# Order of the input and weight loads in a fused gated-attention and ReGLU kernel, and the planner's account of its DMA queues

## The chip, the core and the metric

The kernel runs on one core of a Trainium2 chip. The engines are named as in the profile: PE (matrix products), DVE and ACT (element-wise work; both read the matrix results in PSUM), POOL (element-wise work in SBUF, and the queue of the weight loads) and SP (the queue of all other transfers). The metric is device time in microseconds (us), the median of several runs. One further execution was profiled, and all durations below come from it.

## The reference, cut to what matters

For 4 batches, 8 heads, 768 steps and head width 48, a state of 48x48 decays by a gate of its own for each row, takes up an outer product, and is read by the query. The result, 3072 tokens of 384 numbers, goes through a ReGLU network of 384 to 1536 to 384.

```python
f = 1.0 / (1.0 + np.exp(-f_logit))
for t in range(S):
    state = f[:, :, t, :, None] * state + np.einsum('bhd,bhe->bhde', k[:, :, t], v[:, :, t])
    y[:, :, t] = np.einsum('bhd,bhde->bhe', q[:, :, t], state)
x = y.transpose(0, 2, 1, 3).reshape(B * S, H * D)
out = (np.maximum(x @ w_gate, 0.0) * (x @ w_val)) @ w_out
```

## The kernel before

**Units.** The 3072 tokens are cut into 24 chunks of 128. Two neighbouring chunks of one batch are a unit; there are 12 units, and `seq` (line 399) sets their order: units 0 to 3 are the first 256 tokens of the four batches, 4 to 7 the next, 8 to 11 the last. A unit needs four loads of 384 KB, f, k, q and v (`load`, line 572). Four buffers of each kind exist, so unit 4 loads into the buffers of unit 0.

**Attention of one unit** (`unit`, line 652). ACT takes the exponential and the logarithm of f (lines 669, 671); PE sums the logs over time (678, 679); ACT takes exponentials of the sums (690, 693, 700); DVE or POOL multiply k and q by them ("hats", 712, 718). The hats are turned either by PE (770, copied to `qkT` by DVE or ACT; units in `pe_hats`) or by a DMA transpose (792). PE makes scores (806), which are masked into `ptm` by DVE (820), or by an ACT copy (815) and a POOL product (817). v is spread into `vpad` (753). PE makes the state's increment (860 or 871), DVE and POOL update the state (638, 643, 646), and PE makes the output (904 or 915), which is copied, or copied and turned by a DMA, into `xT` (926, 932 to 934).

**The network** works on groups of four chunks (two units). `ffn_hidden` (line 940) makes, for one of 12 slices j of 128 hidden columns, the gate product (3 matmuls, line 956), its ReLU on ACT (958), the value product (960) and the product `gT` on DVE (964). `ffn_out` (line 969) multiplies by `w_out` (984). For group 0 the loop of line 1015 does some slices in two halves, chunks 0 and 1 (unit 0) first, then chunks 2 and 3 (unit 1), so that half of the work can begin when only unit 0 is done. Gate and value results share four PSUM banks (group "f" in line 463), so PE can be two slices ahead of ACT and DVE.

**The weights** are cast to bf16 on the way in, so POOL issues them (`load_w`, line 585): four slices each of `wg`, `wv` and `wo`, each of three hidden columns j, 288 KB written.

**The order of the work** is not written by hand: a list scheduler inside the kernel (`Plan.schedule`, line 192) has a cost and a priority for every operation and puts each engine's instructions in a fixed order when the kernel is built. On the chip each engine runs its list in order and waits on semaphores; if one instruction waits, everything behind it on that engine waits too. The class `Rings` (line 53) is the scheduler's account of the two DMA queues: `hw` is SP's, `sw` is POOL's. The list `first` (line 398) is the order of the first 16 input loads and 12 weight slices; `wg0@k1` means that the issue of wg0 waits until k1 has landed. A transfer after 30 us is planned as if it landed `op.slack` later (line 1014), a reserve. While PE is planned to wait before 24 us, it is given matmuls on zeros (line 1050; below: fillers) that keep it busy and give nothing.

Of the kernel before, what the change touches and what calls it, by code (L numbers as in the profile page):

```python
# [52 lines left out]
class Rings:  # L53


    CAP, LAND = 3300, 1.0
    RATE = {"hw": (1.0, 0.21), "sw": (1.0, 0.69)}
# [3 lines left out]
    def __init__(self):  # L61
        self.now = 0.0
        self.passed = 0
        self.coming = []
# [13 lines left out]
    def speed(self, ring):  # L78
        return self.RATE[ring][1 if self.queue[self.OTHER[ring]] else 0]

    def worked(self, t, ring):
        work = t - self.now
        if ring == "sw":
            return work
        for p in self.PAUSES[self.passed:]:
            if p >= t:
                break
            work -= max(0.0, min(t, p + self.PAUSE) - max(self.now, p))
        return work

    def later(self, work, ring):
        t = self.now
        if ring == "sw":
            return t + work
        for p in self.PAUSES[self.passed:]:
            if t + work <= p:
                break
            work -= max(0.0, p - t)
            t = max(t, p + self.PAUSE)
        return t + work  # L100

    def next(self):
        found = None
        for r, q in self.queue.items():
            if q:
                t = self.later(self.left[r] / self.speed(r), r)
                if found is None or t < found[0]:
                    found = (t, r)
        if self.coming and (found is None or self.coming[0][0] < found[0]):
            found = (self.coming[0][0], None)  # L110
        return found

    def step(self, t, ring):
        speeds = {r: self.speed(r) for r in self.RATE}
        for r, q in self.queue.items():
            if q:
                self.left[r] -= self.worked(t, r) * speeds[r]
        self.now = t
        while self.passed < len(self.PAUSES) and self.PAUSES[self.passed] + self.PAUSE <= t:
            self.passed += 1  # L120
        if ring is None:
            _, _, op = self.coming.pop(0)
            q = self.queue[op.ring]
            q.append(op)
            if len(q) == 1:
                self.left[op.ring] = op.flow
            return None
        op = self.queue[ring].pop(0)
        self.out[ring] -= op.descs
        if self.queue[ring]:  # L130
            self.left[ring] = self.queue[ring][0].flow
        return op


class Plan:
# [56 lines left out]
    def schedule(self, banks):  # L192
# [46 lines left out]
        while True:  # L239
# [130 lines left out]
def bass_hgrn2_outer__then__ffn_reglu_kernel(  # L370
# [53 lines left out]
    vrow = [sb(f"vrow{i}", [128, 2, HD], BF16) for i in range(2 if any(e.get("vpe") for e in {0: {'kps': False, 'qps': False, 'q0': 'POOL', 'q1': 'POOL', 'even': 'PE', 'm00': 'DVE', 'm01': 'DVE', 'm10': 'DVE', 'tk': 'DVE', 'm11': 'DVE', 'r1': 'POOL', 'tq': 'ACT', 'v11': 'ACT', 'v10': 'DVE', 'r0': 'ACT', 'v01': 'ACT', 'v00': 'DVE1', 'vb': 'DVE1', 'pr': False, 'o1': 'DVE', 'vc0': 'DVE', 'x0': 'ACT', 'x1': 'ACT', 'yy': True, 'o0': 'ACT', 'vc1': 'ACT'}, 1: {'kps': True, 'r0': 'ACT', 'm01': 'DVE', 'm00': 'DVE', 'tq': 'DVE', 'v11': 'POOL', 'even': 'PE', 'tk': 'ACT', 'q1': 'DVE', 'v00': 'DVE1', 'm11': 'POOL', 'r1': 'DVE', 'm10': 'DVE', 'v01': 'POOL', 'v10': 'POOL', 'q0': 'POOL', 'qps': False, 'yy': False, 'td': False, 'vb': 'DVE', 'vc0': 'DVE', 'o0': 'DVE', 'vc1': 'DVE', 'x0': 'ACT', 'o1': 'ACT'}, 2: {'tk': 'DVE', 'v01': 'POOL', 'kps': True, 'r1': 'ACT', 'r0': 'ACT', 'even': 'PE', 'q0': 'DVE', 'v00': 'POOL', 'v10': 'ACT', 'm00': 'DVE', 'v11': 'DVE1', 'm01': 'POOL', 'm11': 'POOL', 'tq': 'DVE', 'q1': 'POOL', 'm10': 'POOL', 'qps': True, 'x0': 'ACT', 'vc1': 'ACT', 'pr': False, 'vc0': 'DVE', 'o0': 'DVE', 'x1': 'ACT', 'vb': 'POOL'}, 4: {'v10': 'DVE1', 'v01': 'POOL', 'm00': 'DVE', 'q11': 'POOL', 'q00': 'POOL', 'q01': 'POOL', 'q0': 'POOL', 'kps': True, 'even': 'DVE', 'm01': 'DVE', 'v00': 'ACT', 'm10': 'POOL', 'q10': 'POOL', 'q1': 'POOL', 'm11': 'POOL', 'v11': 'DVE1', 'qps': False, 'tq': 'DVE', 'r0': 'ACT', 'tk': 'DVE', 'r1': 'ACT', 'yy': True, 'o1': 'ACT', 'o0': 'DVE', 'x1': 'DVE', 'x0': 'DVE'}, 10: {'m00': 'POOL', 'm10': 'POOL', 'q0': 'POOL', 'kps': True, 'q10': 'POOL', 'm01': 'POOL', 'q11': 'POOL', 'q00': 'POOL', 'v11': 'ACT', 'even': 'DVE', 'v01': 'DVE1', 'v00': 'POOL', 'q01': 'POOL', 'q1': 'POOL', 'm11': 'DVE', 'v10': 'ACT', 'td': True, 'o0': 'DVE'}, 9: {'v11': 'ACT', 'v10': 'ACT', 'even': 'DVE', 'kps': True, 'q1': 'POOL', 'm10': 'DVE', 'v00': 'ACT', 'm11': 'POOL', 'q11': 'POOL', 'm00': 'DVE', 'q00': 'POOL', 'q10': 'POOL', 'q0': 'POOL', 'q01': 'POOL', 'v01': 'DVE1', 'm01': 'DVE', 'yy': False, 'x0': 'DVE', 'td': True, 'o0': 'DVE'}, 3: {'kps': True, 'm00': 'DVE', 'm11': 'POOL', 'v11': 'DVE1', 'm10': 'POOL', 'tk': 'ACT', 'v01': 'DVE1', 'r1': 'DVE1', 'tq': 'DVE', 'q1': 'POOL', 'v00': 'DVE1', 'v10': 'POOL', 'q0': 'POOL', 'r0': 'DVE1', 'm01': 'DVE', 'even': 'DVE', 'qps': False, 'vb': 'DVE1', 'x1': 'ACT', 'o1': 'DVE', 'vc1': 'ACT', 'pr': False, 'vc0': 'DVE', 'o0': 'ACT'}, 5: {'q1': 'POOL', 'm00': 'DVE', 'kps': True, 'q11': 'POOL', 'v10': 'ACT', 'v00': 'DVE1', 'even': 'DVE', 'q01': 'POOL', 'm11': 'POOL', 'q00': 'POOL', 'q0': 'POOL', 'v11': 'POOL', 'm01': 'DVE', 'q10': 'POOL', 'v01': 'ACT', 'm10': 'DVE', 'tq': 'ACT', 'r0': 'DVE1', 'tk': 'DVE', 'r1': 'DVE1', 'qps': False, 'o1': 'ACT', 'x0': 'DVE', 'o0': 'ACT', 'yy': False}, 11: {'q0': 'POOL', 'v01': 'ACT', 'q10': 'POOL', 'm00': 'DVE', 'q01': 'POOL', 'm11': 'POOL', 'q1': 'POOL', 'q00': 'POOL', 'kps': True, 'v11': 'ACT', 'm01': 'DVE', 'q11': 'POOL', 'even': 'DVE', 'v00': 'DVE1', 'm10': 'POOL', 'v10': 'DVE1', 'yy': True, 'o1': 'DVE', 'td': True}, 7: {'v10': 'POOL', 'kps': True, 'q1': 'POOL', 'v01': 'POOL', 'q11': 'POOL', 'm00': 'DVE', 'v11': 'DVE1', 'even': 'PE', 'm10': 'POOL', 'm11': 'DVE', 'm01': 'POOL', 'q10': 'POOL', 'qps': False, 'q01': 'POOL', 'q0': 'POOL', 'o0': 'DVE', 'x1': 'DVE', 'td': True, 'x0': 'ACT', 'o1': 'ACT'}, 8: {'m10': 'DVE', 'v11': 'ACT', 'q01': 'POOL', 'm01': 'POOL', 'even': 'DVE', 'q0': 'POOL', 'v10': 'ACT', 'q1': 'POOL', 'm00': 'DVE', 'kps': True, 'q11': 'POOL', 'q00': 'POOL', 'qps': False, 'v00': 'DVE1', 'q10': 'POOL', 'v01': 'ACT', 'pr': False, 'td': True, 'x0': 'DVE'}, 6: {'v10': 'DVE1', 'v01': 'DVE1', 'q10': 'DVE', 'm10': 'DVE', 'kps': True, 'q1': 'DVE', 'even': 'PE', 'q01': 'POOL', 'm00': 'POOL', 'm01': 'POOL', 'q11': 'DVE', 'q00': 'DVE', 'm11': 'POOL', 'qps': True, 'q0': 'DVE', 'pr': False, 'o0': 'DVE', 'yy': False, 'o1': 'DVE'}}.values()) else 0)]  # L424
# [38 lines left out]
    pl = Plan({'bc': 3, 'tp': 1, 's': 4, 'y': 3, 'kv': 4, 'f': 4, 'hot': 1, 'vp': 1})  # L463
    pl.EASY = 30
# [5 lines left out]
    def pe_t(*cols):  # L470
        return sum(max(n, 60) / 2400.0 + 0.0025 for n in cols)
# [671 lines left out]
```

## Time and profile before

| what | value |
|---|---|
| median of 3 runs | 195.18 us (194.57 to 195.86) |
| the profiled execution, own time | 193.87 us |
| its span, first to last instruction | 192.1 us |
| busy: PE, DVE, ACT, POOL | 183.4, 129.2, 121.6, 82.5 us |
| granted PE clock | 1.00 throughout |
| DMA | 31.90 MB, mean 166 GB/s |

The profile's page lists busy time by engine, the span in 40 slices of 4.8 us, the chain of work that ended last, and groups of equal instructions by line. A busy time of one matmul includes its way through the array, and several overlap; what a matmul adds to a sequence has to be read from stretches in which PE worked without a break. In rows of the timeline the two first numbers are the start and the length in us, and a bracket names what the engine had waited for.

### The profile page before, as it was taken

To read this page: it belongs to the slowest core of one execution; us is meant where nothing else is said; L and a number is where in the kernel's file an instruction comes from. 1 tells how busy PE (TensorE), PEld (TensorE's weight loads), DVE (VectorE), ACT (ScalarE), POOL (GpSimd) and SP (SyncE) were. 2 spreads that over 40 slices of the span, in tenths; PEclk is the share of its full clock that TensorE was granted. 3 is DMA by queue.
4 is the path that set the end of the run, shared out by engine and by line. 5 is a ranking of instruction groups with operands and counts; after the bars stand their busy time and mean duration, and the time that the engine had idled before them with its cause. 6 is when DMAs were issued, how large, how long until landed. Compare 5 with 4: busy or idle time off the path is not lost.

```text
span 192.1 us, 4498 instructions
## 1 busy us (share of the span) xinstructions
PE 183.4 (95%) x1755; PEld 101.6 (53%) x1777; DVE 129.2 (67%) x238; ACT 121.6 (63%) x233; POOL 82.5 (43%) x110
## 2 busy tenths in 40 slices
PE   7897899999999999999999999999999999999995
PEld 2355584555654546554655556555555455554564
DVE  4579876778798999994689999553485613444311
ACT  4888868785779989948999357456252553333311
POOL 5379867362435257725878695124040600000000
PEclk9999999999999999999999999999999999999999
DMA  5999999999999999998698975422209110111114
GB/s 154 325 325 274 214 205 205 204 230 248 235 311 285 207 320 232 309 239 160 172 258 230 172 154 118 84 77 61 62 5 149 41 44 0 41 43 41 43 42 123
DMA packets 79089, 31.90 MB, mean 166 GB/s; under 512 B 71254, under 2 KB 79068, under 8 KB 79068
## 3 DMA queue, kind: packets, MB, share of 16 engines
q1 hardware_dynamic: 74268, 28.08, 60.8%
q0 software_dynamic: 4800, 3.54, 11.8%
q8 instruction: 14, 0.23, 0.5%
q14 instruction: 7, 0.06, 0.1%
HBM read 25.96 MB, written 4.73 MB: 160 GB/s over the span
## 4 chain that ended last, share of the span: by engine, by line
PE 71%; DMA 12%; DVE 8%; POOL 4%; issue 2%; ACT 1%; SPq 1%; DVEq 0%
PE ps L952 37%; PE ps L980 23%; DMA wo<-in_moe_w_out_dram 10%; PE ps L806 3%; DMA v_in<-in_v_dram 2%; DVE hats L718 2%; PE ps L904 2%; DVE gT L964 1%; DVE hats L712 1%; DVE ptm L820 1%; POOL wo L606 1%; PE ps L770 1%; PE ps L860 1%; POOL hats L712 1%; PE ps L915 1%
## 5 line engine op out<-in xcount | busy, mean ns | idle before, releaser
L964 DVE TENSOR_TENSOR gT<-relu,ps 128x512 bf16<-128x512 bf16 (+1 forms) x75 | 49.5, 664 | 36.1 <-PE ps L952 29.5
L958 ACT ACTIVATE relu<-ps 128x512 bf16<-128x512 f32 (+1 forms) x75 | 43.4, 580 | 28.4 <-PE ps L952 27.8
L952 PE MATMUL ps<-xT,wv 128*128 128x512 bf16 (+1 forms) x223 | 58.8, 370 | 0.9 <-DMA wv<-in_moe_w_val_dram 0.7
L952 PE MATMUL ps<-xT,wg 128*128 128x512 bf16 (+1 forms) x207 | 55.4, 370 | 1.4 <-issue 0.5
L980 PE MATMUL ps<-wo,gT 128*128 128x384 bf16 (+2 forms) x300 | 51.6, 320 | 0.1
L980 PEld LDWEIGHTS ps<-wo,gT 128*128 128x128 bf16 x300 | 28.2, 98 | 19.5 <-DMA wo<-in_moe_w_out_dram 0.3
L817 POOL TENSOR_TENSOR ptm<-ptm,seen 128x512 bf16<-128x512 bf16 x21 | 23.9, 1154 | 20.8 <-ACT ptm L815 20.7
L952 PEld LDWEIGHTS ps<-xT,wv 128*128 128x128 bf16 x225 | 21.0, 98 | 22.2 <-DVE hats L712 0.8
L952 PEld LDWEIGHTS ps<-xT,wg 128*128 128x128 bf16 x225 | 20.9, 98 | 20.5
L646 POOL TENSOR_TENSOR st<-ssum,dec 128x384 bf16<-128x384 f32 x16 | 13.2, 828 | 24.7 <-DMA dec<-rates 12.0
L504 ACT ACTIVATE osb<-ps 128x384 f32<-128x384 f32 x13 | 6.3, 488 | 20.2 <-PE ps L980 20.2
L820 DVE TENSOR_TENSOR ptm<-ps,seen 128x512 bf16<-128x512 f32 x27 | 17.1, 684 | 2.2 <-PE ps L806 2.1
L718 POOL TENSOR_TENSOR hats<-q_in,expo 64x384 bf16<-64x384 f32 x16 | 15.9, 994 | 5.6 <-ACT expo L693 4.6
L718 DVE TENSOR_TENSOR hats<-k_in,ps 64x384 bf16<-64x384 f32 x28 | 15.4, 552 | 1.1 <-ACT ps L700 0.6
L712 POOL TENSOR_TENSOR hats<-q_in,expo 128x384 bf16<-128x384 f32 x11 | 10.9, 1005 | 11.5 <-ACT expo L693 11.5
L815 ACT ACTIVATE ptm<-ps 128x512 bf16<-128x512 f32 x21 | 11.5, 599 | 2.5 <-PE ps L806 2.5
L505 DVE COPY osb<-ps 128x384 f32<-128x384 f32 (+2 forms) x12 | 6.3, 523 | 9.9 <-PE ps L980 9.8
L502 DVE TENSOR_REDUCE vpad<-v_in 64x384 bf16<-64x384 f32 x17 | 9.3, 545 | 4.3 <-DMA v_in<-in_v_dram 3.6
L693 ACT ACTIVATE expo<-ps 128x384 f32<-128x384 f32 x20 | 9.1, 492 | 4.6 <-DVE ps L682 3.9
L669 ACT ACTIVATE f_in<-f_in 128x768 f32<-128x768 f32 x12 | 10.1, 841 | 1.1 <-DMA f_in<-in_f_logit_dram 1.0
L700 ACT ACTIVATE ps<-ps 128x384 f32<-128x384 f32 x22 | 10.3, 491 | 0.0
L671 ACT ACTIVATE bneg<-f_in 128x768 bf16<-128x768 f32 x12 | 10.1, 842 | 0.1
(86 smaller groups left out, 185.9 us busy)
## 6 DMA issues: line engine op xcount, KB each, us to landing
f_in<-in_f_logit_dram SPq DMA_DIRECT2D x12, 384.0 KB, 5.2
k_in<-in_k_dram SPq DMA_DIRECT2D x12, 384.0 KB, 4.9
v_in<-in_v_dram SPq DMA_DIRECT2D x12, 384.0 KB, 5.6
q_in<-in_q_dram SPq DMA_DIRECT2D x12, 384.0 KB, 4.9
out_dram<-osb SPq DMA_DIRECT2D x15, 192.0 KB, 2.4
out_dram<-osb SPq DMA_DIRECT2D x16, 96.0 KB, 2.2
wg<-in_moe_w_gate_dram POOLq DMA_DIRECT2D x4, 288.0 KB, 9.8
wv<-in_moe_w_val_dram POOLq DMA_DIRECT2D x4, 288.0 KB, 9.7
```

The costliest lines, as they stand in the source:

```text
L646: add(e, lambda: engine[e].tensor_tensor(t4(s_new), t4(tmp), rate, ALU.mult), [key] + dk, [f"S{b}_{y}"], prio=P + 2, **(dict(occ=0.79, lat ...
L669: add("ACT", lambda cut=cut: sc.activation(raw["f"][:, cut], raw["f"][:, cut], AF.Exp, scale=-1.0), [f"f{li}"], [f"f{li}"], prio=P, **act_ ...
L700: add("ACT", lambda i=i, ex=ex: sc.activation(bc[i].ap[:, 0:HD] if in_place else ex[:, 1, :], bc[i].ap[:, 0:HD], AF.Exp, scale=1.0), [bc[i ...
L712: add(e, lambda i=i, n=n, x=x, e=e, exps=exps: engine[e].tensor_tensor(hats[:, hi, i, x, :, 0:D], by_i[n][:, i, :, :], exps(), ALU.mult), ...
L718: op = add(e, lambda i=i, n=n, x=x, e=e, y=y, lo=lo, exps=exps: engine[e].tensor_tensor(hats[64 * i:64 * i + 64, hi, y, x, :, 0:D], by_i[n ...
L815: add("ACT", lambda pt=pt, s=sj[j]: sc.activation(pt, s.ap[:, :].rearrange("p (n t) -> p n t", n=NP), AF.Copy), [sj[j]], [f"raw{mis[y]}_{j ...
L817: add("POOL", lambda pt=pt, mask=mask: gp.tensor_tensor(pt, pt, mask, ALU.mult), [f"raw{mis[y]}_{j}", "seen"], [f"raw{mis[y]}_{j}", f"ptm{ ...
L820: add("DVE", lambda pt=pt, mask=mask, s=sj[j]: ve.tensor_tensor(pt, s.ap[:, :].rearrange("p (n t) -> p n t", n=NP), mask, ALU.mult), [sj[j ...
L952: mm = te.matmul(bank.ap[:, 0:n], wt[:, kt, j * 128:(j + 1) * 128], xT[xi][:, kt, n0:n1], start=(kt == 0), stop=(kt == NK - 1))
L958: add("ACT", lambda: sc.activation(relu[ri][:, 0:n], gate.ap[:, 0:n], AF.Relu), [gate], [f"relu{ri}"], prio=P, **act_t(n))
L964: add("DVE", lambda: ve.tensor_tensor(gT[gi][:, j, n0:n1], relu[ri][:, 0:n], val.ap[:, 0:n], ALU.mult), [val, f"relu{ri}"], [f"gT{gi}_{j}_ ...
L980: mm = te.matmul(bank.ap[:, 0:cut[1] - cut[0]], gT[gi][:, j, r * C:(r + 1) * C], wo[:, j, cut[0]:cut[1]], start=(j == 0), stop=(j == NJ - 1))
```

## The change

Only the order of work changes; what is computed does not. The diff has these parts:

- `first`: in the new order SP loads f0, k1, k0, q0, v0, f1, v1, q1 (units 0 and 1), and the eight gate and value slices are issued behind the landing of q0, f0, v0, f1, k0 and q1. The load of f2 waits until the slice wv2 has landed, and the other loads of units 2 and 3 follow. The output slices wait for f3, v3 and k3. In the old order 13 input loads were issued ahead of the first weight slice.
- `Rings`: the shares of the two queues when both are busy are 0.208 and 0.668 (were 0.21 and 0.69); a first stretch of the POOL queue has shares of its own (`COLD`); a pause of SP's queue no longer stops it but makes a lag, which is added to when a load has landed (`extra`).
- Priorities: the network's operations have P + 1000 instead of P + 60, so the scheduler takes one only where no attention operation is ready at that time.
- The reserve `op.slack` of a transfer is 0.5 instead of 1.5 us.
- Group 0 does five slices by halves instead of three: `range(0, 5)`.
- Unit 5 is no longer in `pe_hats`; `pe_x` and `q_lined` have other members; the table that gives each unit's operations to engines, the table `pace` and the small changes of priorities have new values. In unit 0 v is now spread by PE from a copy made by POOL (`vpe`), q's exponentials go to PSUM and its hats to DVE, and one of its four masks (m01) goes to ACT and POOL; all four were on DVE.

```diff
 class Rings:
-    CAP, LAND = 3300, 1.0
-    RATE = {"hw": (1.0, 0.21), "sw": (1.0, 0.69)}
+    CAP, LAND, SPREAD, INSIDE = 3300, 1.0, 0.45, 0.3
+    RATE = {"hw": (1.0, 0.208), "sw": (1.0, 0.668)}
+    COLD = {"hw": (1.0, 0.36), "sw": (0.83, 0.53)}
...
+    def passing(self, t):
+        v = self.speed("hw")
+        if not self.queue["hw"]:
+            self.lag = max(0.0, self.lag - (t - self.now) * v)
+        while self.passed < len(self.PAUSES) and self.PAUSES[self.passed] < t:
+            if self.queue["hw"] and self.PAUSES[self.passed] >= self.now:
+                self.lag += self.PAUSE * v
+            self.passed += 1
+
+    def extra(self, ring):
         if ring == "sw":
+            return 0.0
+        work, beside, slow = self.SPREAD + self.lag, 0.0, self.RATE["hw"][1]
+        if self.queue["sw"]:
+            beside = self.left["sw"]
+            for op in self.queue["sw"][1:]:
+                beside += op.flow
+            beside /= self.RATE["sw"][1]
+        return (work / slow if work / slow <= beside else beside + work - slow * beside) - self.INSIDE
...
-                    op.end = event[0] + rings.LAND + (op.slack if op.start > self.EASY else 0.0)
+                    op.end = event[0] + rings.LAND + rings.extra(op.ring) + (op.slack if op.start > self.EASY else 0.0)
...
-    first = 'f0 k0 v0 q0 v1 f1 q3 q1 k1 wg0@k1 wv0@k0 wg1@f0 wv1@k0 wg2@f0 wv2@q0 wg3@q3 wo0@k0 wv3@f0 q2 wo2@q2 wo3@k0 wo1@f1 f2 k2 f3 k3@wg0 v2 v3'.split()
+    first = 'f0 k1 k0 q0 wg0@q0 wv0@f0 wg1@f0 v0 wg2@v0 f1 wv1@f1 wv2@k0 wg3@q0 v1 q1 wv3@q1 f2@wv2 q2 k2@wg1 v2@wv2 f3@wg1 wo1@f3 q3@wv0 v3 wo0@v3 k3@wv0 wo2@k3 wo3@k3'.split()
-    pe_hats = {0, 1, 2, 3, 5}
-    pe_x = {0, 1, 2, 3, 4, 5, 7, 8, 9, 10, 11, 12, 13, 15, 22, 23}
-    q_lined = {0, 1, 3, 5, 7, 8, 9, 10}
+    pe_hats = {0, 1, 2, 3}
+    pe_x = {0, 1, 2, 3, 4, 5, 6, 7, 9, 10, 11, 14, 15, 18, 19, 22, 23}
+    q_lined = {0, 1, 4, 6, 8, 10}
...
         chain("ffn", "PE", proj(gate, wg), xk + [slice_of("wg", j)], [gate], occ=pe_t(n, n, n), lat=PE_L,
-              prio=P + 60, opens=[gate])
+              prio=P + 1000, opens=[gate])
...
-                op.slack = 1.5 if op.flow is not None else 0
-        for r0, r1, js in {0: [(0, 2, range(0, 3)), (2, 4, range(0, 3)), (0, 4, range(3, 12))]}.get(g, [(0, GC, range(NJ))]):
+                op.slack = 0.5 if op.flow is not None else 0
+        for r0, r1, js in {0: [(0, 2, range(0, 5)), (2, 4, range(0, 5)), (0, 4, range(5, 12))]}.get(g, [(0, GC, range(NJ))]):
...
-    pace = {6: 21, 10: 24, 5: 3, 8: 31, 9: 23, 11: 49}
+    pace = {4: 1, 10: 24, 3: 1, 11: 47, 5: 10, 6: 13}
```

The built instruction lists show what this moves. PE's list has 32 fillers, 33 before. Before, one gate product stands ahead of unit 1's second output, and all other network products stand behind it. After, eight gate and value products of the first half stand ahead of unit 1's first output, and the first gate product stands ahead of the second transposes of unit 1. On POOL the slices wg0 and wv0 come first, then the copy of v0, wg1 and wg2, a copy of v1, wv1 and wv2, the update of unit 0's state and the mask m01 of unit 0. Before, POOL's first slice stood behind unit 0's q hats and a copy of v1.

More of the change, by code (lines that the diff above doesn't have):

```diff
@@ L63, in __init__ @@
         self.passed = 0
+        self.lag = 0.0
+        self.cold = False
         self.coming = []
@@ L78, in speed @@
     def speed(self, ring):
-        return self.RATE[ring][1 if self.queue[self.OTHER[ring]] else 0]
-    def worked(self, t, ring):
-        work = t - self.now
-        if ring == "sw":
[L84 to L100, printed above, removed]
+        return (self.COLD if self.cold else self.RATE)[ring][1 if self.queue[self.OTHER[ring]] else 0]
+    def passing(self, t):
[7 more added lines that the diff above has]
+    def extra(self, ring):
+        if ring == "sw":
+            return 0.0
[6 more added lines that the diff above has]
+        return (work / slow if work / slow <= beside else beside + work - slow * beside) - self.INSIDE
     def next(self):
@@ L105, in next @@
             if q:
-                t = self.later(self.left[r] / self.speed(r), r)
+                t = self.now + self.left[r] / self.speed(r)
                 if found is None or t < found[0]:
@@ L576, in load @@
         dst = bass.AP(tensor=t, offset=0, ap=[[2 * HD, 128], [2 * D, H], [1, 2 * D]])
-        behind = list(after) + (sent[-8:][:1] if len(sent) >= 8 else [])
+        behind = list(after) + (sent[-4:][:1] if len(sent) >= 4 else [])
         op = chain("load", "SP", lambda: sy.dma_start(dst, src), [], [f"{n}{u % NL}"], occ=0.65, lat=1.3, prio=u * 20 - 40, after=behind)
```

39 lines of the change are left out of this document (21 added, 18 removed).

## The prediction

> **What bounds the kernel now.** I read the page first, then PE's timeline up to 24 us, then the chain, then the DMA queues in windows.
>
> ```profile
> span 192.1 us, 4498 instructions
> PE 183.4 (95%) x1755; PEld 101.6 (53%) x1777; DVE 129.2 (67%) x238; ACT 121.6 (63%) x233; POOL 82.5 (43%) x110
> PE   7897899999999999999999999999999999999995
> PE 71%; DMA 12%; DVE 8%; POOL 4%; issue 2%; ACT 1%; SPq 1%; DVEq 0%
> ```
>
> PE is the bound: only the first five slices, 4.8 us each, and the last show it less than 90% busy, and 71% of the chain that ended last is its own. But fillers count as busy, so the timeline must say when useful work is steady.
>
> ```profile
> 1.66 3.84 PE L1050 MATMUL ps<-zeros 128*128 128x512 bf16 x10
> 12.33 0.62 PE L806 MATMUL ps<-qkT 48*128 48x128 bf16 x16
> 15.31 0.41 PE L904 MATMUL ps<-ptm,vpad 128*32 128x128 bf16 x16
> 21.65 0.50 PE L952 MATMUL ps<-xT,wg 128*128 128x256 bf16 x3
> 23.32 0.49 PE L952 MATMUL ps<-xT,wv 128*128 128x256 bf16 x3 [0.66 <-DMA wv<-in_moe_w_val_dram]
> ```
>
> Unit 0's scores stand at 12.33 and its output at 15.31; network products run without a break from 23.32, after a wait for a slice. How much work is that? The chain in order of time gives what a matmul adds to a full PE:
>
> ```profile
> 46.55 0.20 PE ps L915 x8
> 47.72 0.45 PE ps L871 x16
> 49.25 0.50 PE ps L904 x28
> 55.77 0.34 PE ps L860 x8
> 63.58 0.45 PE ps L770 x8
> 64.78 0.20 PE ps L847 x8
> 161.82 3.88 PE ps L952 x18
> 165.71 1.95 PE ps L980 x12
> 181.92 7.84 PE ps L980 x60
> ```
>
> So 3.88/18 = 0.216 us for 512 columns, 1.95/12 = 0.163 for 384, 0.056 for a transpose (L770), 0.028 and 0.043 for the two kinds of state matmuls (L871, L860), 0.018 and 0.025 for the two kinds of outputs (L904, L915). Multiplying the built list's counts by such pitches gives 172.4 us of useful work in all, of which 8.3 lie before 23.32. PE therefore loses 23.3 - 8.3 = 15.0 us in the head, and 181.92 + 7.84 - 172.4 = 17.4 us until its last matmul: 2.4 us are lost after the head, and what is left of the span is the last copy and store.
>
> **The sum of PE's work does not change.** Unit 5 gives up 16 transposes (-0.89) and 16 state matmuls of 0.028 (-0.45) for 8 of 0.043 (+0.34); its totals come back to PE (9 as in L847, +0.22); unit 0's spread of v adds 4 of 384 columns (+0.65); one more output is made by 16 narrow matmuls (+0.29) and not 8 (-0.20); 24 half products replace 12 full ones (24 x 0.109 - 12 x 0.216 = +0.02). Together -0.02 us. The time moves only by waits, so the sum is one over losses, place by place.
>
> **Landings.** The rates of the two queues:
>
> ```profile
> 3.00:15.00 12.00, 10.79 (x100) 5.23 (x99) 6.80 (x14) 9.59 (x19) 5.90 (x13) 1.00 1.17 324
> DMA packets 845, 0.60 MB, mean 202 GB/s; under 512 B 79, under 2 KB 845, under 8 KB 845
> q0 software_dynamic: 797, 0.59, 127.3%
> ...
> DMA packets 6102, 3.48 MB, mean 205 GB/s; under 512 B 3110, under 2 KB 6098, under 8 KB 6098
> q0 software_dynamic: 3116, 2.30, 86.4%
> q1 hardware_dynamic: 2982, 1.13, 37.8%
> ```
>
> The first row (stretch, length, busy time of PE, PEld, DVE, ACT and POOL, clock, DMA share, GB/s) is SP's queue alone: 324 GB/s, so a load of 0.393 MB takes 1.21 us. The next two (21 to 24 us) are nearly POOL's queue alone: a slice of 0.295 MB takes 1.50 us. The last three (26 to 41 us) are both: the slice gets 2.30/3.48 of 205 GB/s, 2.2 us, and the load 1.13/3.48 of it, 5.9 us.
>
> ```profile
> 14.22 0.93 POOL L606 DMA_DIRECT2D wg<-in_moe_w_gate_dram  x1 [1.08 <-DMA k_in<-in_k_dram]
> f_in<-in_f_logit_dram SPq DMA_DIRECT2D x1, 384.0 KB, 11.3
> wg<-in_moe_w_gate_dram POOLq DMA_DIRECT2D x1, 288.0 KB, 6.7
> DMA to landing us min/median/max: 3.4/5.2/17.9
> ```
>
> f0, first on SP's list, lands 3.4 us (the last row, that of f) after its issue at 0.8; q0, three loads later, at 4.2 + 3 x 1.21 = 7.9, as q0 does now. So wg0 is issued at 8.2, 6.0 us earlier than now (14.22), and lands at 8.2 + 6.7 = 14.9. Behind it come wv0, wg1, wg2, wv1, wv2. Between 1.5 and 2.2 us each I take 1.7, nearer the lone queue, because SP's list runs dry after q1: wv1 at 21.7, wv2 at 23.3; at 2.2 us wv2 would land at 25.9. The first six loads come at 1.21 us each, f1 at 10.3. The last two meet the first slices. Now, a load issued just before wg0 (the f row, issued at 13.93) took 11.3 us; moved by 6.0 that is q1 at 19. If its last packets do not straggle, its bytes at the rates above are in by 16. I take 17, and v1 at 12.5 (12 to 13).
>
> **Unit 0 and unit 1.** Scores of unit 0 wait, as now, for ACT's copy behind the exponential of f1 (10.3): 12.3, unchanged. But the mask m01 now ends on POOL, behind the copy of v1, two issues, a state update and its own product.
>
> ```profile
> 15.14 0.78 POOL L606 DMA_DIRECT2D wv<-in_moe_w_val_dram  x1
> 20.06 0.82 POOL L646 TENSOR_TENSOR st<-ssum,dec 128x384 bf16<-128x384 f32 x1 [0.83 <-DVE ssum L643]
> 18.82 0.56 DVE L638 TENSOR_TENSOR st<-ps,dec 128x384 bf16<-128x384 f32 x1
> 20.86 1.15 POOL L817 TENSOR_TENSOR ptm<-ptm,seen 128x512 bf16<-128x512 bf16 x1
> 19.89 1.88 DVE L820 TENSOR_TENSOR ptm<-ps,seen 128x512 bf16<-128x512 f32 x3
> 24.23 0.78 DVE L964 TENSOR_TENSOR gT<-relu,ps 128x256 bf16<-128x256 bf16 x2
> 13.59 0.87 ACT L693 ACTIVATE expo<-ps 128x384 f32<-128x384 f32 x2 [0.59 <-PE ps L679]
> 15.77 1.06 ACT L504 ACTIVATE xT<-ps 128x384 bf16<-128x384 f32 x2 [0.45 <-PE ps L904]
> ```
>
> From v1's 12.5: 0.7 (wait and copy) + 2 x 0.78 + 0.82 + 1.15 = 16.7, where DVE's four masks end by 15.3 now, when the output starts. Queued behind POOL's wait for v1 are also wv1, wv2 and unit 0's state: each us that v1 is late is a us for them and, through wv2, for f2. So unit 0's output is 1.4 us later, its two ACT copies (1.06) end at 18.5, and the first gate product starts at 18.5, not 21.65: 3 us earlier. Unit 1's scores follow, behind three slices' products, at 20.7. Then DVE has three masks (1.88), the state (0.56), a sum and two copies of x (as long as the state, by size), behind two of its gT (0.78): 4.5 us with waits: unit 1's x is whole at 25.3 (24.5 to 26.1), where the halves of unit 0 are used up. PE has done 11.0 us of work by then: a loss of 14.3 (13.5 to 15.1). Against 15.0 now that is **-0.7 us**. What comes late next is x, not the weights.
>
> **f2 behind wv2.** SP issues f2 at 23.3; alone it needs 3.4 us, so 26.7. ACT has its exponential ahead of the eighth ReLU, whose bank PE needs for the tenth half, after 13.6 us of work. An exponential of 768 columns (estimated as the 0.87 of two of 384, L693), a ReLU of half width and hand-overs, 1.4 us, must fit before: PE stalls if f2 lands after 14.3 + 13.6 - 1.4 = 26.5. Cost +0.2, taken as **0** since x's bounds are wider; at the slow end (wv2 at 25.9, f2 at 29.3) +2.8. Its cover is the 24 half products; SP has q2, k2 and v2 queued behind f2, and they wait with it.
>
> **Units 2 and 3 in one burst.** With P + 1000 ACT has four exponentials and a copy (some 0.44 each, L693) between the ReLUs of slices 5 and 6, and again before that of slice 9; DVE has the hats and spreads of unit 2 and later of unit 3 ahead of those slices' gT.
>
> ```profile
> 60.00:85.00 25.00, 24.41 (x292) 13.46 (x296) 24.08 (x44) 22.60 (x42) 13.60 (x17) 1.00 1.10 273
> ```
>
> PE may be two slices (2.6 us) ahead; each burst is 3 to 4 us on an engine, so up to 1 us is lost at each of two places. Now the stretch to 55.77 costs 1.0 (39.8 us of work lie before it, a loss of 16.0). I take 1.8, so **+0.8** (0 to +2.2).
>
> **Output slices.** The loads from f2 to v3, six later, end at 26.7 + 6 x 1.21 = 34; wo0, behind v3, lands about 7 us later as the first slice does, at 41.3; PE comes to it at 14.3 + 27.1 + 0.8 = 42.2: 0. The cover is 0.9 us; without it each us that v3 is late is a us of PE. **From 50 us on.** DVE is full from 60 to 85 us (24.08 of 25 in the window's row), and PE waits for it there. Up to the 25th gT the new list has 53.4 us of DVE work where PE has 51.9; the old 52.2 where PE has 54.2. DVE is 3.5 us nearer to being the bound: **+0.3** (-0.5 to +1.5). The dropped reserve of 1 us on transfers moves issues, costs no instruction, and is in that range. The tail is the same instructions.
>
> Sum: -0.7 + 0 + 0.8 + 0 + 0.3 = +0.4 us. The profiled execution took 193.87, so it would take 194.3; it stands 1.3 us (0.7%) below the median of 195.18, so the median comes to **195.6 us**, for the likeliest case 193.5 to 197.0.
>
> **A rule against the change.** Fillers before 5 us ran at 3.84/10, 0.38 us each, 512 columns later take 0.216, and the wait of 0.66 us in the row at 23.32 slowed nothing. In the new head PE waits about 1 us behind its nine fillers for m01. The Trainium skill (TensorE: Matmul & The Clock Gate, Part 1) says that after an idle window of some 3.4 us the array runs at half clock. By that rule 1 us costs nothing, and this trace, with 1.00 throughout, agrees so far; only if the mask came past 19 us would it bite.
>
> **Rivals.** (1) *Burst decides, slower:* if both bursts block PE by their full length less the two slices, with DVE waits in between, they cost 2 x 1.6 for the 1.0 now, and DVE's stretch +0.8: -0.7 + 2.2 + 0.8 = +2.3, 197.5 us. For it: 24.08 of 25 us of DVE; against: three output projections follow that DVE need not keep up with. It decides once unit 2's sums come later than 31 us. Chance 0.18. (2) *The phases do not hold:* POOL's slices keep the mixed pace, f2 lands at 29.3: +0.4 + 2.8 = +3.2, 198.4. For it: the slices' even 2.2 us now; against: SP's queue is empty meanwhile. 0.10. (3) *Faster:* q1 at 16 and v1 at 12 and DVE keep unit 1's x ahead of the halves, the loss stays at unit 0's 12.9, and there is no burst stall: -2.1 - 0.5 = -2.6, 192.6. For it: the first gate product 3 us earlier; against: DVE's 4 us. 0.24. (4) *The clock drops* for one 3.4 us window, half of which is lost: +1.7 + 0.4, 197.3. 0.02. The forecast keeps 0.46.
>
> **Chances.** Within 1% (1.95 us, about what a measurement of this kernel can tell from no change): 0.46. Faster: 0.24 (rival 3). Slower: 0.18 + 0.10 + 0.02 = 0.30. The range 192.6 to 198.4 reaches to rivals 3 and 2 and leaves half of each outside, under 0.2.
>
> **What would show it.** Right: first gate product at 18 to 19 us; q1 at 16 to 18; PE idle before unit 1's halves with DVE's xT as releaser; waits of PE for ACT's ReLU at 34 to 42 us. Wrong: network products without a break from 20 us (rival 3), ACT idle on f2 past 27 us (rival 2), PE's 512-column matmuls at twice 0.216 us (rival 4), DVE as chain for over 10 us between 50 and 95 us (rival 1).

## The result, and the profile after

| what | kernel before | changed kernel |
|---|---|---|
| median, 20 runs each | 194.39 us (193.66 to 195.86) | 196.22 us (195.0 to 199.0) |
| ratio to before | | 1.0085, 95% interval 1.0062 to 1.0108 |
| the profiled execution, own time | 193.87 us | 195.76 us |
| its span | 192.1 us | 194.0 us |
| granted PE clock | 1.00 | 1.00 |

The changed kernel is 0.85% slower, about 1.65 us. The ratios, here and below, leave out the runs that lie over 1.5% above the fastest of their kernel, and the medians keep them. The forecast was 0.4 us, without a measurable difference. From here on line numbers are those of the changed kernel, five above those of the kernel before.

The page after: span and instructions, busy time, PE in 40 slices, shares of the chain that ended last.

```profile
span 194.0 us, 4529 instructions
PE 186.0 (96%) x1785; PEld 101.6 (52%) x1785; DVE 130.9 (67%) x245; ACT 119.6 (62%) x233; POOL 81.5 (42%) x110
PE   7899989989999999799999999999999999999995
PE 62%; DMA 20%; DVE 9%; issue 3%; POOL 2%; SPq 2%; ACT 2%; DVEq 0%
```

PE is still the bound, but its share of the chain fell from 71% to 62% and that of the DMA rose from 12% to 20%. The slices show where: one 8 in the sixth (24 us) and the ninth (39 to 43 us) and a 7 in the 17th (78 to 82 us), which was a 9 before.

PE's timeline after, at unit 0's output, at the first gate product and at the main waits behind it:

```profile
16.47 0.41 PE L909 MATMUL ps<-ptm,vpad 128*32 128x128 bf16 x16 [0.29 <-POOL ptm L822]
18.05 0.50 PE L957 MATMUL ps<-xT,wg 128*128 128x256 bf16 x3
24.77 0.50 PE L957 MATMUL ps<-xT,wg 128*128 128x256 bf16 x3 [0.70 <-DVE xT L510]
29.02 0.34 PE L683 MATMUL ps<-bneg,upto 128*128 128x384 bf16 x1 [0.15 <-ACT bneg L676]
39.11 0.82 PE L957 MATMUL ps<-xT,wv 128*128 128x512 bf16 x3 [0.33 <-DVE ssum L648]
42.93 1.15 PE L985 MATMUL ps<-wo,gT 128*128 128x384 bf16 x6 [0.60 <-DMA wo<-in_moe_w_out_dram]
76.98 0.82 PE L957 MATMUL ps<-xT,wg 128*128 128x512 bf16 x3 [0.26 <-DVE xT L510]
82.12 0.62 PE L811 MATMUL ps<-qkT 48*128 48x128 bf16 x16 [1.07 <-DMA qkT<-hats]
```

The longest of these waits, 1.07 us, is at 82.12: the scores of unit 6 wait for its transposes.

To compare two lists in another order I count, for each matmul, the useful work ahead of it (instructions by the pitches of the prediction) and subtract that from its start. The difference is what PE has lost by then. All work is 172.4 us in both.

| useful work done, us | 5 | 20 | 27 | 36 | 60 | 64 | 100 | end |
|---|---|---|---|---|---|---|---|---|
| time of that point after, us | 17.0 | 34.1 | 42.0 | 52.0 | 76.4 | 82.1 | 118.6 | 191.5 |
| lost before, us | 12.58 | 15.11 | 15.23 | 15.92 | 16.09 | 16.10 | 17.16 | 17.16 |
| lost after, us | 12.03 | 14.07 | 15.03 | 15.96 | 16.42 | 18.09 | 18.63 | 19.06 |
| difference | -0.55 | -1.04 | -0.20 | +0.04 | +0.33 | +1.99 | +1.47 | +1.90 |

So the head wins 1.04 us. The stretch from 34 to 42 us gives 0.84 back, that to 52 us another 0.24, and from there the loss grows to 1.90, the difference of the spans. The jump is between 76 and 82 us. The chain that ended last, in order of time, shows what led to it:

```profile
56.95 0.69 DVE gT L969
...
75.88 0.45 DVE xT L510
76.33 5.74 DMA qkT<-hats
82.07 0.05 issue
82.12 0.62 PE ps L811 x16
```

The chain lies on DVE from 56.95 to 76.33 and then on one transpose of 5.74 us. There are two readings: DVE is the bound and delivers late, or the transpose is late by itself. SP's timeline and one row of DVE, with two instructions, tell more (start, length, engine, line, operation):

```profile
70.69 2.96 SPq L939 DMA_TRANSPOSE xT<-xn  x1
73.69 1.31 SPq L797 DMA_TRANSPOSE qkT<-hats  x1
75.04 0.58 SPq L583 DMA_DIRECT2D k_in<-in_k_dram  x1
75.67 0.62 SPq L583 DMA_DIRECT2D q_in<-in_q_dram  x1
76.33 3.40 SPq L797 DMA_TRANSPOSE qkT<-hats  x1
```

```profile
70.46 1.14 DVE L723 TENSOR_TENSOR hats<-q_in,ps 64x384 bf16<-64x384 f32 x2
```

Unit 6's last hats are done at 71.6 on DVE, 4.7 us before its second transpose is issued. Ahead of it on SP's list stand a transpose of xn, whose issue lasts until 73.65, unit 6's first transpose, and the loads k and q of unit 8. Its own issue takes 3.40 us instead of 1.31. It lands at 76.33 + 5.74 = 82.07.

### The profile page after: what moved, and what is told of

Read it like the earlier page. It is cut to its first block, busy times and chain, and to the rows that moved or that the text cites. A ratio compares the mean times of both kernels' runs of the same rounds, so it can differ in the third digit from the quotient of the medians.

```text
span 194.0 us, 4529 instructions
## 1 busy us (share of the span) xinstructions
PE 186.0 (96%) x1785; PEld 101.6 (52%) x1785; DVE 130.9 (67%) x245; ACT 119.6 (62%) x233; POOL 81.5 (42%) x110
## 4 chain that ended last, share of the span: by engine, by line
PE 62%; DMA 20%; DVE 9%; issue 3%; POOL 2%; SPq 2%; ACT 2%; DVEq 0%
PE ps L957 31%; PE ps L985 23%; DMA wv<-in_moe_w_val_dram 5%; DMA wo<-in_moe_w_out_dram 4%; DVE gT L969 3%; DMA v_in<-in_v_dram 3%; DMA k_in<-in_k_dram 3%; DMA qkT<-hats 3%; DVE hats L723 3%; DMA q_in<-in_q_dram 3%; PE ps L811 2%; PE ps L909 2%; SPq L583 2%; DVE ptm L825 1%; POOL wg L611 1%
## 5 line engine op out<-in xcount | busy, mean ns | idle before, releaser
L957 PE MATMUL ps<-xT,wg 128*128 128x512 bf16 (+1 forms) x231 | 59.3, 365 | 1.0 <-DVE xT L510 1.0
L822 POOL TENSOR_TENSOR ptm<-ptm,seen 128x512 bf16<-128x512 bf16 x26 | 29.5, 1154 | 28.2 <-ACT ptm L820 28.2
L509 ACT ACTIVATE osb<-ps 128x384 f32<-128x384 f32 (+2 forms) x18 | 8.5, 472 | 22.6 <-PE ps L985 22.6
L723 DVE TENSOR_TENSOR hats<-k_in,ps 64x384 bf16<-64x384 f32 x32 | 17.6, 551 | 1.9 <-ACT ps L705 1.2
L820 ACT ACTIVATE ptm<-ps 128x512 bf16<-128x512 f32 x26 | 14.2, 595 | 4.2 <-PE ps L811 4.2
L825 DVE TENSOR_TENSOR ptm<-ps,seen 128x512 bf16<-128x512 f32 x22 | 14.2, 682 | 0.3 <-PE ps L811 0.2
L705 ACT ACTIVATE ps<-ps 128x384 f32<-128x384 f32 x24 | 11.3, 493 | 0.0
L1055 PE MATMUL ps<-zeros 128*128 128x512 bf16 x32 | 9.4, 441 | 0.1
L698 ACT ACTIVATE expo<-ps 128x384 f32<-128x384 f32 x16 | 7.3, 495 | 3.0 <-DVE ps L687 3.0
L510 POOL CAST vpad<-v_in 64x384 bf16<-64x384 f32 x13 | 6.5, 498 | 5.9 <-DMA v_in<-in_v_dram 5.2
```

Source lines behind the costliest of these rows:

```text
L705: add("ACT", lambda i=i, ex=ex: sc.activation(bc[i].ap[:, 0:HD] if in_place else ex[:, 1, :], bc[i].ap[:, 0:HD], AF.Exp, scale=1.0), [bc[i ...
L723: op = add(e, lambda i=i, n=n, x=x, e=e, y=y, lo=lo, exps=exps: engine[e].tensor_tensor(hats[64 * i:64 * i + 64, hi, y, x, :, 0:D], by_i[n ...
L820: add("ACT", lambda pt=pt, s=sj[j]: sc.activation(pt, s.ap[:, :].rearrange("p (n t) -> p n t", n=NP), AF.Copy), [sj[j]], [f"raw{mis[y]}_{j ...
L822: add("POOL", lambda pt=pt, mask=mask: gp.tensor_tensor(pt, pt, mask, ALU.mult), [f"raw{mis[y]}_{j}", "seen"], [f"raw{mis[y]}_{j}", f"ptm{ ...
L825: add("DVE", lambda pt=pt, mask=mask, s=sj[j]: ve.tensor_tensor(pt, s.ap[:, :].rearrange("p (n t) -> p n t", n=NP), mask, ALU.mult), [sj[j ...
L957: mm = te.matmul(bank.ap[:, 0:n], wt[:, kt, j * 128:(j + 1) * 128], xT[xi][:, kt, n0:n1], start=(kt == 0), stop=(kt == NK - 1))
```

## The experiments

Seven of the twelve kernels (1, 2 and 8 to 12) keep the plan of the changed kernel and edit its finished lists; five were planned anew. With `behind`, added after `pl.schedule`, instructions of SP are issued behind a later one:

```diff
+    def behind(name, at, names):
+        line = order["SP"]
+        last = line[at]
+        moved = [line[n] for n in names]
...
+        for n, op in enumerate(moved):
+            op.start = last.start + 0.01 * (n + 1)
+        rest = [op for op in line if op not in moved]
+        cut = rest.index(last) + 1
+        order["SP"] = rest[:cut] + moved + rest[cut:]
...
```

**1. Unit 8's loads behind unit 6's transpose.**

```diff
+    behind("qkT2_c1", 45, [43, 44])
```

> The changed kernel with one edit after its plan is made: on SP the loads k and q of unit 8 are issued behind unit 6's second transpose instead of ahead of it; nothing else moves. Theory (SP's queue): the two loads put two transfers of about 1.1 us each ahead of that transpose, so it lands about 2 us earlier than 82.07, the wait of 1.07 us of unit 6's scores goes, and the span falls from 194.0 to about 192.9: ratio to the kernel before about 1.003 (1.0085 for the changed kernel). Rival (VectorE is full from 56 to 83 us and sets the pace): TensorE waits as long a little later, on rows released by DVE, the span stays within 0.3 of 194.0 and the ratio at 1.007 to 1.010.

Measured: 195.24 us, ratio 1.0047 (1.0021 to 1.0072), span 193.5. SP and PE now:

```profile
70.93 1.86 SPq L939 DMA_TRANSPOSE xT<-xn  x1
72.84 2.69 SPq L797 DMA_TRANSPOSE qkT<-hats  x2
75.56 0.58 SPq L583 DMA_DIRECT2D k_in<-in_k_dram  x1
```

```profile
80.83 0.62 PE L811 MATMUL ps<-qkT 48*128 48x128 bf16 x16
...
107.55 0.40 PE L811 MATMUL ps<-qkT 48*128 48x128 bf16 x8 [0.31 <-DVE gT L969]
```

Both transposes are issued in 2.69 us, by 75.53, and the scores start at 80.83 without a wait, 1.29 us earlier; PE had been 0.15 ahead at 76.83 already, so 1.14 is the edit's. DVE's list is the same, so it was not DVE that held them: the first reading falls for this place, SP's order is the cause. The profile's list of waits had put 2.3 us of the long issue at 76.33 down to a sum on DVE that ended at 78.57. Here the same sum ends at 78.42, after the transposes are issued, so they do not need it. Runs 8, 9, 11 and 12 keep this edit, and in all of them the scores start without a wait, in run 9 although the first transpose was issued later (74.22) than in the changed kernel. But of the 1.29 us only 0.5 remain at the end: 0.5 is given back at 107.55, at a new wait, and 0.2 at about 114 us.

**2. wo0 ahead of wo1 on POOL.** PE reads wo0 first, but the plan loads wo1 first.

```diff
+    first_out, second_out = done["wo1"], done["wo0"]
...
+    for field in ("deps", "start", "end", "pos", "users"):
+        a, b = getattr(first_out, field), getattr(second_out, field)
+        setattr(first_out, field, b)
+        setattr(second_out, field, a)
+    order["POOL"].sort(key=lambda op: op.pos)
```

> The changed kernel with the first two output slices exchanged in POOL's queue and the plan otherwise as it was: wo0, which the output product reads first, takes the place, the waits and the time of wo1. Theory (order in the queue): wo0 lands at about 39.2 instead of 42.88, the wait of 0.60 us at 42.93 goes, and the span falls by 0.6 to 0.76 us, ratio about 1.005. Rival (covered elsewhere, or wo1 is needed as soon): the same wait moves to wo1 a few products later, the span falls by less than 0.2 us, ratio 1.008.

Measured: 196.41 us, ratio 1.0102 (1.0052 to 1.0152). wo0 landed at 39.15 and nothing waited for it, but the first output product started at 42.85 instead of 42.93:

```profile
38.64 0.82 PE L957 MATMUL ps<-xT,wg 128*128 128x512 bf16 x3 [0.24 <-DVE st L643]
39.79 0.82 PE L957 MATMUL ps<-xT,wv 128*128 128x512 bf16 x3 [0.33 <-DVE ssum L648]
...
42.85 1.14 PE L985 MATMUL ps<-wo,gT 128*128 128x384 bf16 x6
```

Waits for DVE, these two and one of 0.33 at 36.47, took the place of the wait for wo0. In this execution v of unit 2 had landed at 32.03 instead of 31.30, and DVE had waited 1.08 us for it (0.20 in the changed kernel), before POOL issued wo0 at 33.44. So the trace does not show that the edit made these waits. The time shows no gain, but with an interval of about 1 us to either side it can't rule out the 0.6 us.

**3. The burst's evictions first** (planned anew).

```diff
-            prio=P, **act_t(n))
+            prio=P - 200 * (g == 0), **act_t(n))
```

and the same for the product gT.

> The changed kernel with ReLU and the gated product of the first group (the first four windows) ahead of all other work in the planner's priorities; planned anew. Theory (the burst of units 2 and 3 delays the evictions that free TensorE's banks): the waits at 29.02 and 39.11, together 0.8 us, shrink by at least 0.5, ratio about 1.005, unless unit 2 then comes late. Rival (ACT and DVE are simply full there, so that order among them gives nothing): the waits move to unit 2's or 3's own products, ratio 1.007 to 1.012.

Measured: 200.53 us, ratio 1.0310 (1.0268 to 1.0353). The rival's side, and far beyond it. Unit 2's scores come earlier (37.99, against 41.16 in the changed kernel), but PE now waits for DVE's other work: 1.17 us for a state at 24.66, 0.67 for a mask at 40.27, and 1.85 for hats at 58.58. Unit 3's scores begin at 49.33 (46.33) and unit 4's at 68.81 (66.10).

```profile
58.58 0.87 PE L957 MATMUL ps<-xT,wg 128*128 128x512 bf16 x2 [1.85 <-DVE hats L723]
59.24 1.49 PE L957 MATMUL ps<-xT,wv 128*128 128x512 bf16 x3
```

The three matmuls at 59.24 take 1.49 us where such a row takes 0.81; more on that at the end.

**4. The old order of loads with all else new** (planned anew: `first` of the kernel before).

> The changed kernel with the order of loads of the kernel before, all else as changed (the new account of the queues, engine choices, units 5 and 6); planned anew. If the new order of loads itself is what costs (burst 0.8, waits for f2 and wo0 1.1, against the head's gain of 1.1 to 1.3): the span is 0 to 1 us below 194.0, ratio 1.003 to 1.009, with the first gate product back at 19 to 20 us. If the engine choices fit only the new order: 1 to 4 us longer than before, ratio 1.01 to 1.02. If later steps (unit 6's transposes) carry the loss, they show the same wait near 82 us here.

Measured: 198.66 us, ratio 1.0219 (1.0178 to 1.0260).

```profile
21.58 0.50 PE L957 MATMUL ps<-xT,wg 128*128 128x256 bf16 x3 [0.45 <-DMA wg<-in_moe_w_gate_dram]
...
81.31 0.40 PE L811 MATMUL ps<-qkT 48*128 48x128 bf16 x8 [1.32 <-DMA qkT<-hats]
```

This is the second of the three cases, a little above its range, and the third as well. The head is as late as in the kernel before (21.65), and the wait for unit 6's transposes is there with the old order too: it belongs to the later choices, not to the order of the first loads.

**5 and 6. The new order alone; the new order with the new account of the queues** (kernel before, planned anew: `first` of the changed kernel; then its `Rings` and `EASY` too).

> The kernel before with the new order of loads alone; its own account of the queues, engine choices and units by DMA stay; planned anew. Theory (the choices fit only the order they were made for, as the kernel with the old order and the new choices showed with 1.0219): 1.01 to 1.03, with new waits between 20 and 60 us. Rival (the new order is good by itself and the new choices brought the loss behind 50 us): the head's gain of about 1 us stays and the burst of 0.8 and wo0's 0.76 take it back, ratio 0.997 to 1.005.

> The kernel before with the new order of loads and the new account of both queues (rates, lag and spread of the landing times), but its old engine choices, priorities and slack; planned anew. If the account is what makes the new order work: ratio 0.003 to 0.01 below the order alone. If the account only shifts the plan's times: within 0.004 of the order alone.

Measured: 201.26 us, 1.0338 (1.0269 to 1.0407), and 203.19 us, 1.0440 (1.0388 to 1.0493). The first lies just above the theory's 1.01 to 1.03. The account did not help the old choices: 0.010 more, which neither expectation had. About 1.7 us of run 6 is a stretch at half clock, told at the end. The longest wait with the order alone, and then with the account:

```profile
59.76 0.59 PE L952 MATMUL ps<-xT,wg 128*128 128x512 bf16 x2 [1.40 <-DMA xT<-xn]
```

```profile
61.79 1.89 PE L775 MATMUL ps<-ident,hats 128*128 128x128 bf16 x16 [2.33 <-DVE hats L717]
```

The order of loads and the choice of engines go together: either half alone is 2.2 to 4.4% slower, both together 0.85%. What a part alone is worth can't be read from such halves, and run 7 shows that planning anew costs as much after a far smaller change.

**7. The reserve for landings back at 1.5 us** (planned anew).

```diff
-                op.slack = 0.5 if op.flow is not None else 0
+                op.slack = 1.5 if op.flow is not None else 0
```

> The changed kernel with the allowance for late landings in the plan put back from 0.5 to 1.5 us; planned anew, unit 6's second transpose still behind the two loads or not as the plan then has it. Theory (the plan put unit 6's scores too close behind their transposes' assumed landing, which was 82.07 on the chip): the scores come later in TensorE's order, the wait of 1.07 goes and the span falls by 0.5 to 1.2, ratio 1.002 to 1.006. Rival (a later place for the scores only moves the wait, or the new plan loses as much elsewhere): ratio 1.008 or more.

Measured: 198.90 us, ratio 1.0212 (1.0161 to 1.0262), on the rival's side. The wait for qkT is gone, but the new plan waits for DVE:

```profile
79.78 0.59 PE L957 MATMUL ps<-xT,wg 128*128 128x512 bf16 x2 [1.37 <-DVE xT L510]
```

Every kernel that was planned anew came out 2.1 to 4.4% slower, whatever was changed. The remaining runs therefore edit the finished lists.

**8. Edits 1 and 2 together.**

> The changed kernel with both queue edits: unit 8's loads k and q behind unit 6's second transpose on SP, and wo0 ahead of wo1 on POOL; the plan otherwise as it was. If the two waits are independent: 1.0047 less 0.6 us for wo0, ratio about 1.002. If wo0's wait is covered by VectorE's delay at 36 to 40 us, as the run with wo0 first alone suggests: about 1.0047, with no wait for wo at 43 us and waits for DVE of the same size ahead of it.

Measured: 195.61 us, ratio 1.0069 (1.0033 to 1.0104). As in 2, the wait for wo0 is gone, v of unit 2 landed late (31.80) and waits for DVE stand ahead; the time shows no gain beside edit 1.

**9. Edit 1, and a second one of its kind.** Unit 10's load v and a store are issued behind unit 8's second transpose.

```diff
+    behind("qkT0_c0", 70, [67, 68])
```

> The run with unit 8's loads moved behind, and a second edit of the same kind on SP: unit 10's load v and one store of the output, which stand ahead of unit 8's second transpose, are issued behind it. In the run without it the wait at 82 us was gone (1.29 us won), but 0.7 us was given back at 105 to 108 us. Theory (that too is SP's queue): the transpose issued at 102.7 comes at about 101, the wait at 107.5 goes, ratio about 1.002. Rival (VectorE, which there waited for unit 10's q, landing at 103.9 in both runs, holds TensorE anyway): ratio stays at 1.0047.

Measured: 195.77 us, ratio 1.0058 (1.0021 to 1.0094), span 193.0. The wait at 107.55 is gone from the trace, as the theory has it, and the span of this one execution is 0.5 us shorter. The time did not follow: the ratios of 1 and 9 can't be told apart.

**10. Two copies of unit 3's values from DVE to POOL.** In the finished lists `vrest0_0` and `vrest0_1` leave DVE and stand behind `hq3_1` on POOL.

```diff
...
+    moved = [order["DVE"][n] for n in (69, 71)]
+    for n, op in enumerate(moved):
...
+        op.eng, op.start, op.end = "POOL", last.start + 0.1 * (n + 1), last.start + 1.0
+        op.emit.__defaults__ = op.emit.__defaults__[:-1] + ("POOL",)
...
```

> The changed kernel with two copies of unit 3's values (0.55 us each, at 36.89 and 37.93 on VectorE) given to POOL, behind its work that ends at about 41.2, where it then waited 1.45 us; the plan otherwise as it was. Theory (VectorE's burst makes the wait at 39.11): that wait goes, but wo0 still lands at 42.9, so the wait for it grows from 0.6 to about 1 us and the span stays: ratio 1.007 to 1.010. Rival (the burst's delay passes on to what follows by itself): 0.4 us or more is won, ratio 1.006 or less.

Measured: 196.06 us, ratio 1.0070 (1.0035 to 1.0105).

```profile
43.52 0.66 PE L985 MATMUL ps<-wo,gT 128*128 128x384 bf16 x3 [1.35 <-DMA wo<-in_moe_w_out_dram]
```

The wait at 39.11 is gone, and the wait for wo0 grows from 0.60 to 1.35 us; 0.6 of that is wo0 itself, which landed that much later in this execution. PE came to it 0.16 us earlier, although f2 had cost it 0.47 more at 29 us. The time can't be told from that of the changed kernel, as the theory has it: at 39 to 43 us the burst on DVE hides behind wo0, and to relieve the burst alone wins nothing. Whether wo0 alone would win its 0.6 us stays open, since v was late in runs 2 and 8.

**11. Edits 1, 2, 9 and 10 together.**

> The changed kernel with all four edits: both moves on SP, wo0 ahead of wo1 on POOL, and unit 3's two copies on POOL; the plan otherwise as it was. Theory (wo0's wait and VectorE's burst cover each other, so that only both edits together win): 0.8 to 1.2 us at 36 to 43 us beside the 1.2 us of the two moves on SP, span about 192, ratio 0.996 to 1.000. Rival (VectorE is the bound from 56 to 108 us): what is won at 43 is given back between 56 and 83 in waits for DVE, ratio 1.002 to 1.005.

Measured: 195.47 us, ratio 1.0055 (1.0023 to 1.0087), span 193.6; the theory's range is missed. The first output product starts at 41.96, 0.82 us ahead of run 1, although v of unit 2 was late again (32.06): together edits 2 and 10 do win at this place, as far as one execution of each can tell. At 104 us 0.56 of it is left, at 110 us none. The chain there:

```profile
101.78 4.06 DMA v_in<-in_v_dram
105.86 0.52 ACT vpad L509
106.38 0.49 ACT relu L963
106.89 0.69 DVE gT L969
```

Unit 10's v, which edit 9 had put back, now lands at 105.84; ACT waits for it with a ReLU queued behind its copy, DVE waits for the ReLU, and PE for the bank that DVE frees. SP issued q and v of unit 10 at these times in the kernel before (first fence) and in the changed kernel (second):

```profile
92.80 0.58 SPq L578 DMA_DIRECT2D q_in<-in_q_dram  x1
93.42 1.46 SPq L578 DMA_DIRECT2D v_in<-in_v_dram  x1
```

```profile
98.16 0.38 SPq L583 DMA_DIRECT2D q_in<-in_q_dram  x1
98.60 0.57 SPq L583 DMA_DIRECT2D v_in<-in_v_dram  x1
```

They are 5 us later in the changed kernel. So SP's list looks like a second gate, which the next run tests.

**12. As 11, with unit 10's q and v issued ahead of a transpose of xn and of unit 8's first transpose.**

```diff
-    behind("qkT0_c0", 70, [67, 68])
+    behind("v2", 67, [64, 65])
+    behind("qkT0_c0", 70, [68])
```

> The run with all four edits, with one place on SP changed: unit 10's loads q and v, which there landed at 103.17 and 105.83 (97.30 and 98.55 in the kernel before), are issued ahead of a transpose of xn and of unit 8's first transpose, instead of behind them. In that run TensorE had won 0.8 us at 43 and kept 0.56 at 104 against the run with one move, and gave 1.2 back at 106 to 108, where ACT and VectorE had waited for these loads. Theory (SP runs its list in order, so the loads of unit 10 arrive late, and this sets the second gate at 107 to 108 us): q lands at about 100, v at about 101, the waits at 106.96 and 107.64 go, span 192.2 to 192.6, ratio 0.998 to 1.002. Rival (VectorE or unit 8's transposes, now later, hold the same place): the waits stay at about 1 us with another releaser, ratio 1.004 to 1.007.

Measured: 195.48 us (193.5 to 198.72), ratio 1.0033 (0.9994 to 1.0072), between the two ranges; span of the profiled execution 191.7. Unit 10's q landed at 99.61 and v at 100.83.

```profile
93.81 0.94 SPq L583 DMA_DIRECT2D q_in<-in_q_dram  x1
94.80 2.39 SPq L583 DMA_DIRECT2D v_in<-in_v_dram  x1
```

```profile
105.39 0.62 PE L811 MATMUL ps<-qkT 48*128 48x128 bf16 x16
```

All 16 score matmuls run without a wait at 105.39, where run 11 had them at 106.96 and 107.64. Of this 0.9 us was there at 76 us already, mostly by loads of unit 2 that landed earlier in this execution (f at 26.73 against 27.21, v at 31.42 against 32.06); the other 1.1 is the edit's, as the theory had it. The interval reaches 1: by this ratio the version is not shown to differ from the kernel before, and it does not beat it; its median is 1.3 us above the 194.14 of before. Its runs spread over 5.2 us, those of the kernel before, beside it, over 2.2 (193.53 to 195.77). Its fastest run equals the fastest of before, so what is left of the loss shows in the spread. Its two longest runs, 198.11 and 198.72, have a mean clock of 0.991, where the others have 1.00: one stretch of 3.4 us at half clock, as told at the end, gives that. What makes the rest of the spread stays open: no run took it apart.

## Why the prediction came out as it did

**PE's work unchanged:** right, 172.4 us in both. One reading of the page was off by a digit: of its first five slices the third is a 9, not below 90%.

**Landings:** right in order, a little too slow. q0 landed at 8.03 (7.9 in the prediction), wg0 at 14.52 (14.9), v1 at 11.61 (12.5), q1 at 15.13 (17, and 16 to 18 as a sign), wv2 at 22.55 (23.3). From wg1 on the slices came 1.3 to 1.5 us apart; I had taken 1.7. So POOL's queue does run alone once SP's is dry, as rival 2 would not have it.

**Head, -0.7:** it was -1.04. Unit 0's output started at 16.47 (16.7); PE waited 0.29 us for its mask, not about 1. The first gate product started at 18.05 (18.5), unit 1's halves at 24.77 (25.3) behind 0.70 us of waiting for DVE's xT, as forecast.

**f2 behind wv2, 0:** f2 landed at 27.09 (26.7), the wait is the 0.15 at 29.02. Right.

**Burst, +0.8:** 0.84 between 34 and 42 us. Right in size. The row at 39.11 names DVE, not ACT's ReLU, which I had looked for.

**Output slices, 0 with a cover of 0.9:** the loads to v3 ended at 35.45 (34), and wo0 landed at 42.88 (41.3). The cover was used up and 0.60 us of waiting came, as the price said. Against the 0.69 that the kernel before lost in the same stretch it is +0.24. Run 10 shows that the burst hides behind it: the two terms must not be added.

**From 50 us on, +0.3 (-0.5 to +1.5):** the step that failed. It was 1.90 - 0.04 = +1.86, outside its own range. I priced the stretch by DVE's work alone and put what moves on SP into the range at no cost of its own. The trace has 1.24 us of the loss (start against start, the wait with its hand-over) at one transpose that stood behind two loads on SP; run 1 removes it with DVE's list untouched. A second gate of the same kind, unit 10's loads issued 5 us later, took back what run 11 had won ahead of it, until run 12 moved them. The rest, some 0.6 us, is not resolved; the wait of 0.26 at 76.98 is a part of it.

**Rivals:** the sign of rival 1, DVE as chain for over 10 us, came (56.95 to 76.33), but its price did not: the chain of run 12 lies on DVE just as long, from 55.36 to 75.33, in a span of 191.7 us. DVE is near the bound there without setting the end. Rivals 2 and 3 did not come. Rival 4 did not come in the profiled execution, but one of the 20 runs, the longest with 199.0 us, has a mean clock of 0.991. The 1.00 of the row for the kernel before holds from 4.7 us on: until then its fillers started 0.43 us apart, twice the later 0.216, and the trace has no record of the clock there. So the 0.38 us of the prediction is a mean of two paces.

The head's gain and the burst were right, and up to 52 us so was their sum (+0.04 against +0.1). Most of the loss behind, 1.24 of 1.86 us in the trace, came from a queue that I had counted for the first 42 us and not behind them. That the time came near the forecast (196.22 against 195.6) is in part luck: the forecast started from a median of three runs, 195.18, and 20 runs gave 194.39. Against that the change is +1.65 us, four times the +0.4, and the interval of 0.23% to either side tells 0.85% from nothing, where the forecast took 1% as about the least that can be told.

## What to carry to other kernels

When a plan moves, read the list of every queue that runs in order to its end, not only where the change is: a transfer that nobody waits for yet still delays a transpose behind it that somebody does wait for. A wait can hide behind a later one, as the burst hid behind wo0, so relieve both before you judge either, and then look for the next gate behind them. To test one edge of a planned kernel, edit the finished lists: here each new plan cost 2.1 to 4.4%, more than any edge was worth. And compare executions before the edited place too: with the same list they differed there by up to 0.9 us.

## What the hardware showed that I had not expected

A DMA transpose issued behind two loads took 3.40 us to issue and 5.74 to land; two in a row without loads between took 2.69 us together (run 1) and landed 3.32 and 4.90 us after they were issued. Runs 2 and 10, which keep the two loads ahead, have 3.88 and 2.56 us for the same issue. What the longer issue waits for stays open.

In run 3 PE stood still for 1.85 us and then ran at half clock. Busy time by stretch, the clock is the third number from the right:

```profile
58.00:59.00 1.00, 0.42 (x2) 0.36 (x4) 0.91 (x2) 0.97 (x2) 0.85 (x3) 0.88 1.14 349
59.00:60.00 1.00, 1.00 (x4) 0.30 (x2) 0.00 (x0) 0.97 (x3) 1.00 (x2) 0.50 1.05 336
...
62.00:63.00 1.00, 1.00 (x14) 0.59 (x13) 0.65 (x2) 0.48 (x1) 0.96 (x2) 0.91 1.41 224
```

The clock was 0.50 from about 58.8 to 62.2, some 3.4 us, which costs 1.7 us on top of the wait. The wait of 2.33 us in run 6 did the same; a wait of 1.56 (run 6, at 46.31) left the clock at 1.00. The length of the wait does not tell it all. In the ten kept traces that record a change of the clock, the changes stand whole multiples of 3.41 us apart (1, 16, 40, 55, 56 and 57 times). So I cut the time into such pieces and read how busy PE was in the one ahead of the change: first run 3 before its drop, then run 6 before its drop, then the piece of run 6 with the wait of 1.56 us.

```profile
55.34:58.76 3.42, 1.25 (x55) 1.02 (x55) 3.12 (x6) 3.38 (x9) 3.12 (x5) 1.00 1.03 285
57.75:61.16 3.41, 1.71 (x39) 1.02 (x26) 2.33 (x5) 2.88 (x8) 1.62 (x3) 1.00 1.16 281
44.10:47.51 3.41, 1.80 (x10) 0.85 (x10) 3.06 (x6) 3.38 (x6) 3.41 (x4) 1.00 1.25 209
```

PE was busy for 1.25 and 1.71 us where the clock then fell, and for 1.80 us where it stayed. So what a wait costs depends also on where it falls in such a piece; three pieces do not fix a threshold. It also bears on the spread of the runs: of the 78 runs of the kernel before that were taken beside runs 1 to 12 none has a mean clock under 0.999, of the 20 of the changed kernel one has 0.991, and of the 76 of the seven kernels with edited lists ten have.

The Trainium skill (TensorE: Matmul & The Clock Gate, Part 1) has the clock halve after an idle window of some 3.4 us and come back after a busy one of that length. The length of the slow stretch agrees, but here a window that was idle for half to two thirds of its length was enough.
